# Attention and a gated MLP on one core: a planner that counts the loads of q and k, and the broadcast of the reciprocals, for longer

## The chip, the cores and the metric

The kernel runs on one core of a Trainium2 chip. The metric is the device time of one execution in microseconds (us), as the median of several executions.

## The reference

Eight batches, eight heads, 576 positions, head size 64. The attention output goes straight into a gated MLP with a mixing over positions. Everything is 32-bit float. Cut to what matters:

```python
q_rot, k_rot = rotate(q), rotate(k)              # rotary embedding over 64 features
scores = matmul(q_rot, k_rot.T) / sqrt(64)
attn = exp(scores - max(scores)); attn /= sum(attn) + 1e-9
x = matmul(attn, v)                              # (8, 576, 512) after heads are joined
h = maximum(x @ w_in, 0); u, v = halves of h     # w_in 512 x 1024
v_n = (v - mean) / sqrt(var + 1e-6)
v_s = einsum('ts,bsd->btd', w_spatial, v_n) + b_spatial
out = (u * v_s) @ w_out
```

## The kernel before

**Tiling.** Two heads of a batch make a *pair*; there are 32 pairs, four to a batch, and after each four an MLP for their batch. Each value that a matmul needs in more precision is split into a rounded high part and the rest, its low part. The scores of a pair are nine tiles of 128 queries by 576 keys (`sc`), each followed by a negated row maximum on VectorE (`nmx`, line 563), an exponential on ScalarE (`e`, line 565) whose row sums go to `sums`, transposes (`tp`) and products with v (`pv`). Pair 0 is treated whole in plain 32-bit float (`prepare_whole`, line 552), pairs 1 to 3 have split scores but plain values (`attention_plain`), and pairs 4 to 31 are split throughout (`attention`).

**The preparation of a pair** (`prepare`). Two loads bring q and k with their swapped halves into two `stage` buffers (`st`, line 409, issued at line 306 like every transfer). Then come, for each of q and k, two products with the rotary tables (line 401, tables `tabq` and `tabs`) and their sum (line 405), the rounding on ScalarE (line 309) and the low part (line 312). Ten transfers inside the chip, the *stack*, then put the parts in place for the scores (`qs`, `ks`, `qz`). There are only two stage buffers, so the loads of a pair wait until the last stack transfer of the pair before has read them; and `qs`, `ks`, `qz` exist once, so a stack waits until TensorE has finished the scores of the pair before.

**The end of a pair** (`normalise`). Once all nine columns of sums are there, VectorE takes the reciprocal (line 711) and transposes it (`rt`, line 712); `put` writes it to DRAM in four transfers; `get` reads it back broadcast to 128 partitions in three (`rb`, line 714). GpSimd then multiplies `x32`, the pair's attention output, by `rb` (line 716). The MLP reads the result.

**The order of the work** comes from a planner that runs when the kernel is built (`Program.run`). Each operation carries a cost in ns for its engine and a key, and a list of what it waits for. The planner walks through time: when an engine is free, it takes, among the operations that are ready and find a buffer, the one with the lowest key. A result counts as there after the cost, the engine's own latency (`LATENCY`, 1700 ns for a transfer, 118 for VectorE, 200 for TensorE) and `late`, an extra that is 0 unless it is set. All transfers share one queue in the plan, one after the other. `pair_op` marks operations that either GpSimd or VectorE may take, VectorE with 10 added to the key (`STEAL`), and in the plan the two never run such operations at the same time; pairs whose key is under `EARLY` (140) offer nearly all of theirs to both. At one instant VectorE is looked at before GpSimd. Only the order that comes out is used: on the chip each engine runs its list in that order and waits at each instruction for what it needs.

**Costs that the prediction uses**: loads of k, the table and q of pair 0 at 1450 each and v at 910, then pair 1's two loads at 1640 each; `turn_k` at 2280, the two parts of `turn_q` at 736 and 1336, a score tile of pair 0 at 1056, `nmx` at 665; a rotary product or sum 668 on VectorE and 1378 on GpSimd; `put` 2600, `get` 2000.

Weight decoding (`decode`) fills VectorE between the pairs up to about 110 us: six VectorE operations and two on ScalarE for each of twelve weight blocks.

Of the kernel before, what the change touches and what calls it, by code (L numbers as in the profile page):

```python
# [29 lines left out]
PE, ACT, DVE, POOL, DMA = "pe", "act", "dve", "pool", "dma"  # L30
LATENCY = {PE: 200, ACT: 142, DVE: 118, POOL: 95, DMA: 1700}
TO_PE = 105
LATE = 1500
SLOTS = {
    "stage": 2, "lk": 1, "vraw": 2, "vs": 2, "e2": 4, "e1": 2, "eh": 7, "rb": 1, "x32": 1, "xg": 7, "m": 4,
    "small": 3, "nmx": 3, "rt": 2, "sc": 2, "pv": 1, "pm": 3,
# [32 lines left out]
K_INV, K_GET, K_X, K_XHI, K_XLO = 15, 21, 26, 24, 27  # L69
# [37 lines left out]
class Program:  # L107
# [5 lines left out]
    def op(self, eng, ns, key, f, r=(), w=(), new=(), port=False):  # L113
        return self.either({eng: ns}, key, lambda e: f(), r, w, new, port)
# [23 lines left out]
    def run(self, make):  # L138
        free = {p: list(range(n)) for p, n in SLOTS.items()}
        ready = {e: [] for e in LATENCY}  # L140

        own = dict.fromkeys(SLOTS, 0)
        for o in self.ops:
# [80 lines left out]
def tile_attention_gated_mlp(  # L224
# [33 lines left out]
    op = prog.op  # L258
    vec = {DVE: nc.vector, POOL: nc.gpsimd}

    def pair_op(n, key, f, pieces=1, first=POOL, **kw):

        costs = {POOL: pool_ns(n) + 150 * (pieces - 1)}
        if first == DVE:
            costs = {DVE: dve_ns(n) + 68 * (pieces - 1)} if key < EARLY else {DVE: dve_ns(n) + 68 * (pieces - 1), **costs}
        elif key < EARLY:
            costs[DVE] = dve_ns(n) + 68 * (pieces - 1)
        prog.either(costs, key, lambda e: f(vec[e]), **kw)
# [36 lines left out]
    def load(dst, src):  # L305
        nc.sync.dma_start(out=dst, in_=src)

    def round_hi(hi, src):
        nc.scalar.activation(hi, src, AF.Copy)  # L309

    def rest_lo(eng, lo, src, hi):
        eng.tensor_tensor(out=lo, in0=src, in1=hi.bitcast(F32), op=ALU.subtract)  # L312
# [68 lines left out]
    def prepare(i):  # L381
        b, hp = pairs[i]
        key = 20 * i
        if i < WHOLE:
            return prepare_whole(i, b, hp, key)
        st = [Buf("stage", [P, 2 * S + TW], F32, f"st{i}_{j}") for j in range(2)]
        lk = Buf("lk", [P, TW + S], F32R, f"lk{i}")
        vr = Buf("vraw", [P, NQ, 2, D], F32, f"vr{i}")
        vs = Buf("vs", [P, NQ, 2, 2, D], F32R, f"vs{i}")
        prepped.append((lk, vr if i < PLAIN else vs))  # L390

        def hi(j, rows=slice(0, P)):

            return st[j][rows, S:2 * S + TW * j].bitcast(F32R)

        def lo_q(e):
            rest_lo(e, st[0][:, :S].bitcast(F32R), st[0][:, :S], hi(0))

        def rope(j, part, eng):
            cols = slice(S * part.start, S * part.stop)  # L400
            f = lambda e: e.tensor_tensor(out=st[j][:, cols], in0=st[j][:, cols], in1=(tabs if j else tabq)[:, cols], op=ALU.mult)  # L401
            pair_op(S * (part.stop - part.start), key - K_ROPE, f, first=eng, r=["tabs" if j else "tabq"], w=[(st[j], c) for c in range(part.start, part.stop)])

        def rope_sum(j, eng):
            f = lambda e: e.tensor_tensor(out=st[j][:, :S], in0=st[j][:, :S], in1=st[j][:, S:2 * S], op=ALU.add)
            pair_op(S, key - K_SUM, f, first=eng, r=[(st[j], 1)], w=[(st[j], 0)])

        for j in range(2):
            o = op(DMA, 1640, key - K_LOAD, lambda j=j: load(st[j][:, :2 * S], qk[b, hp, j].rearrange("p c n -> p (c n)")), w=[(st[j], 0), (st[j], 1)], new=[st[j]])
            o.late = LATE if i >= 4 else 0  # L410
        op(DMA, 910, key - K_LOAD + 1, lambda: load(vr.tile, v[b, hp]), w=[vr], new=[vr])
        for j, eng, part in ROPE0 if b == 0 else ROPE:
            if part is None:
                rope_sum(j, eng)
            else:
                rope(j, slice(*part), eng)
        op(ACT, 573, key - K_HIQ, lambda: round_hi(hi(0), st[0][:, :S]), r=[(st[0], 0)], w=[(st[0], 1)])
        pair_op(S, key - K_LOQ, lo_q, r=[(st[0], 1)], w=[(st[0], 0)])

        def hi_k():  # L420
            round_hi(hi(1)[:, TW:], st[1][:, :S])
            round_hi(hi(1)[:, :TW], st[1][:, 4 * P:S])

        def lo_k(e):
            rest_lo(e, lk[:, TW:], st[1][:, :S], hi(1)[:, TW:])
            rest_lo(e, lk[:, :TW], st[1][:, 4 * P:S], hi(1)[:, :TW])

        op(ACT, 720, key - K_HIQ, hi_k, r=[(st[1], 0)], w=[(st[1], 1)])
        pair_op(S + TW, key - K_LOK, lo_k, pieces=2, r=[(st[1], 0), (st[1], 1)], w=[lk], new=[lk])
        for a in range(2):  # L430
            own = slice(64 * a, 64 * a + 64)
            oth = slice(64 - 64 * a, P - 64 * a)
            qd, kd = qs[a][:, a * TW:a * TW + S], ks[a]
            zd = qz[:, a * S:a * S + S]
            for dst, rows, j, part, tok in (
                (qd, own, 0, 1, ("qs", a, 0)), (kd, own, 1, 1, ("ks", a, 0)), (kd, oth, 1, 1, ("ks", a, 1)),
                (zd, own, 0, 1, ("qz", a)), (qd, oth, 0, 0, ("qs", a, 1)),
            ):
                op(DMA, 650, key - (K_STACK2 if a else K_STACK), lambda dst=dst, rows=rows, j=j, part=part, own=own: load(dst[rows, :].bitcast(F32), hi(j, own).bitcast(F32) if part else st[j][own, :S]), r=[(st[j], part)], w=[tok])
        if i < PLAIN:  # L440
            return
        op(ACT, 627, key + K_V, lambda: round_hi(vs[:, :, :, 0, :], vr.tile), r=[vr], w=[(vs, 0)], new=[vs])
        pair_op(2 * NQ * D, key + K_VLO, lambda e: e.tensor_tensor(out=vs[:, :, :, 1, :], in0=vr.tile, in1=vs[:, :, :, 0, :].bitcast(F32), op=ALU.subtract), r=[vr, (vs, 0)], w=[(vs, 1)])
# [245 lines left out]
    def normalise(i, sm, x32, key):  # L689
        rt = Buf("rt", [P, 32], F32, f"rt{i}")  # L690
        rb = Buf("rb", [P, S], F32, f"rb{i}")
        x = Buf("xg", [P, 2 * S + TW], F32R, f"x{i}")
        xs.append(x)
        need = [("sums", i % 2, c) for c in range(9)]

        def put():
            for j in range(4):
                load(rt.scratch[:, 32 * j:32 * j + 32], rt[32 * j:32 * j + 9, :])

        def get():  # L700
            row = rt.scratch.rearrange("t p -> (t p)").rearrange("(o n) -> o n", o=1)
            load(rb[0:64, :], row[:, :S].to_broadcast([64, S]))
            load(rb[64:P, 4 * P:], row[:, S:S + TW].to_broadcast([64, TW]))
            load(rb[64:P, :4 * P], row[:, S + TW:].to_broadcast([64, 4 * P]))

        def low(e):
            rest_lo(e, x[:, S + TW:], x32.tile, x[:, :S])
            rest_lo(e, x[:, S:S + TW], x32[:, 4 * P:], x[:, 4 * P:S])

        op(ACT, 100, key + K_INV, lambda: nc.scalar.activation(sm[:, 0:9], sm[:, 0:9], AF.Copy, bias=1e-9), w=need)  # L710
        op(DVE, 130, key + K_INV, lambda: nc.vector.reciprocal(out=sm[:, 0:9], in_=sm[:, 0:9]), w=need)
        op(DVE, 125, key + K_INV, lambda: nc.vector.transpose(out=rt.tile, in_=sm), r=need, w=[rt], new=[rt])
        op(DMA, 2600, key + K_INV, put, r=[rt], w=[(rt, 1)])
        op(DMA, 2000, key + K_GET, get, r=[(rt, 1)], w=[rb], new=[rb])
        whole = [(x32, c) for c in range(len(CHUNKS))]
        pair_op(S, key + K_X, lambda e: e.tensor_tensor(out=x32.tile, in0=x32.tile, in1=rb.tile, op=ALU.mult), r=[rb], w=whole)  # L716
        op(ACT, 573, key + K_XHI, lambda: round_hi(x[:, :S], x32.tile), r=whole, w=[(x, 0)], new=[x])
        pair_op(S, key + K_XLO, low, pieces=2, r=[*whole, (x, 0)], w=[(x, 1)])
# [142 lines left out]
    for n in range(0):  # L861
        idle = Buf("pv", None, None, f"idle{n}")
        wide = lambda: ident.rearrange("p (o n) -> p o n", o=1).to_broadcast([P, 4, P])
        op(PE, 1600, 10000 + n, lambda idle=idle: nc.tensor.matmul(idle.tile.rearrange("p (c n) -> p c n", c=4), lhsT=ident, rhs=wide(), start=True, stop=True), r=["ident"], w=[idle], new=[idle])
    prepare(0)
    for c in range(4):
        decode(DEC_V[c], win, (1, c), w_in[c * P:(c + 1) * P, 2 * HF:4 * HF])
# [7 lines left out]
    for i in range(len(pairs)):  # L875
        if i:
            prepare(i)
        (attention_plain if i < PLAIN else attention)(i)
        if i % NP == NP - 1:
            mlp(i // NP)  # L880
# [68 lines left out]
```

## Time and profile before

| | |
|---|---|
| median of 3 executions | 967.62 us (966.43 to 967.69) |
| the profiled execution | 965.91 us, its span 964.0 us |
| TensorE busy | 933.5 us, 97% of the span |
| ScalarE, VectorE, GpSimd busy | 738.9, 670.5, 576.8 us |
| granted TensorE clock | 1.0 throughout |

The span goes from the first to the last instruction; some 1.9 us of the profiled execution lie outside it. PE is TensorE's matmuls, PEld its weight loads, DVE is VectorE, ACT ScalarE, POOL GpSimd, and SPq the queue that issues all transfers. TensorE's busy time counts overlapping matmuls once.

### The profile page before, as it was taken

The page shows a single profiled execution, that of the slowest core. Times are in us where ns is not written, and L with a number is a line of the kernel's source. Part 1 is how long each engine was busy: PE and PEld are TensorE (multiplying, and loading weights), DVE is VectorE, ACT ScalarE, POOL GpSimd, SP SyncE. Part 2 cuts the span into 40 slices and gives each one's busy share as a digit, 9 for nine tenths or more (in the row PEclk, how much of TensorE's full clock was granted, in tenths as well). Part 3 has the DMA queues.
Part 4 walks back from the last instruction along what each step waited for, and adds up shares of the span by engine and source line. Part 5 has one row for each costly group of instructions (what it writes and reads, how often), then busy time and mean ns, then how long its engine had stood idle before and what let it go on. Part 6 is the DMA issues. An engine that isn't in the chain of part 4 may idle for free.

```text
span 964.0 us, 19475 instructions
## 1 busy us (share of the span) xinstructions
PE 933.5 (97%) x6614; PEld 853.2 (89%) x6614; DVE 670.5 (70%) x1478; ACT 738.9 (77%) x1840; POOL 576.8 (60%) x504
## 2 busy tenths in 40 slices
PE   4988999999999999999999999999999999999998
PEld 2555689999899989999899998999889998999998
DVE  6999797766866677666776668676686766866331
ACT  4887798777987779777897779877798678976452
POOL 5566454566767657775765766666586775672121
PEclk9999999999999999999999999999999999999999
DMA  7786643455354654346444444445524455430101
GB/s 269 243 244 173 167 123 109 131 135 144 93 141 112 168 145 105 108 115 175 126 131 126 115 148 117 127 122 152 145 76 132 125 165 146 104 88 13 62 1 50
DMA packets 56037, 124.64 MB, mean 129 GB/s; under 512 B 13185, under 2 KB 13441, under 8 KB 55938
## 3 DMA queue, kind: packets, MB, share of 16 engines
q1 hardware_dynamic: 55938, 123.40, 46.4%
q8 instruction: 53, 0.87, 0.4%
q14 instruction: 46, 0.38, 0.1%
HBM read 66.03 MB, written 9.58 MB: 78 GB/s over the span
## 4 chain that ended last, share of the span: by engine, by line
PE 71%; ACT 14%; DVE 8%; DMA 3%; issue 2%; POOL 1%; SPq 1%; ACTq 0%; DVEq 0%
PE pc L791 12%; PE sc L542 12%; PE pv L606 11%; PE tp L582 11%; PE pd L806 10%; PE pb L773 9%; ACT e L565 4%; PE pa L750 4%; DVE nmx L563 2%; ACT eh L593 2%; ACT vv L837 2%; DVE el L312 1%; PE pv L679 1%; ACT vv L824 1%; ACT st L309 1%
## 5 line engine op out<-in xcount | busy, mean ns | idle before, releaser
L593 ACT ACTIVATE eh<-tp 128x384 fp32r<-128x384 f32 (+1 forms) x504 | 217.8, 434 | 87.7 <-PE tp L582 70.8
L312 DVE TENSOR_TENSOR el<-tp,eh 128x384 fp32r<-128x384 f32 x336 | 185.5, 553 | 99.6 <-ACT eh L593 87.6
L563 DVE TENSOR_REDUCE nmx<-sc 128x1 f32<-128x576 f32 x288 | 214.9, 749 | 39.9 <-PE sc L542 35.2
L565 ACT ACTIVATE e<-sc,nmx 128x576 f32<-128x576 f32 x288 | 213.4, 741 | 36.5 <-DVE nmx L563 33.7
L582 PE MATMUL tp<-ident,e 128*128 128x128 f32 (+1 forms) x1176 | 195.8, 273 | 3.2 <-DVE eh L312 1.3
L401 POOL TENSOR_TENSOR st<-st,tabq 128x576 f32<-128x576 f32 x58 | 82.1, 1432 | 150.1 <-DMA st<-in_qk_dram 115.8
L582 PEld LDWEIGHTS tp<-ident,e 128*128 128x128 f32 (+1 forms) x1176 | 145.3, 138 | 19.0 <-issue 4.0
L606 PE MATMUL pv<-eh,vs 128*128 128x384 f32 (+1 forms) x560 | 154.4, 316 | 0.4 <-ACT x L685 0.2
L791 PE MATMUL pc<-wsp,vn 128*128 128x288 f32 x768 | 143.3, 303 | 0.5 <-DVE u L853 0.5
L773 PE MATMUL pb<-x,wi 128*128 128x288 f32 x768 | 141.8, 306 | 1.0 <-DVE eh L312 0.7
L806 PE MATMUL pd<-g,wo 128*128 128x288 f32 x768 | 141.3, 303 | 0.0
L542 PE MATMUL sc<-ks,qs 128*128 128x288 f32 x620 | 132.1, 302 | 2.3 <-ACT e L565 2.2
L750 PE MATMUL pa<-wi,x 128*128 128x512 f32 x448 | 133.0, 407 | 0.9 <-POOL x L312 0.5
L542 PE MATMUL sc<-lk,qz 128*128 128x288 f32 x558 | 119.5, 295 | 0.0
L791 PEld LDWEIGHTS pc<-wsp,vn 128*128 128x128 f32 x768 | 114.9, 189 | 2.8 <-DVE u L853 0.9
L806 PEld LDWEIGHTS pd<-g,wo 128*128 128x128 f32 x768 | 114.2, 189 | 3.2 <-DVE el L312 0.2
L773 PEld LDWEIGHTS pb<-x,wi 128*128 128x128 f32 x768 | 112.0, 189 | 4.5 <-PE pb L773 1.3
L606 PE MATMUL pv<-el,vs 128*64 128x384 f32 (+1 forms) x448 | 113.7, 294 | 0.0
L542 PEld LDWEIGHTS sc<-ks,qs 128*128 128x128 f32 x620 | 99.7, 188 | 13.3 <-ACT e L565 5.8
L606 PEld LDWEIGHTS pv<-eh,vs 128*128 128x128 f32 x560 | 97.7, 188 | 6.5 <-DVE x L621 1.6
L716 POOL TENSOR_TENSOR x<-x,rb 128x576 f32<-128x576 f32 x32 | 45.8, 1431 | 84.4 <-DVE x L621 81.0
L312 DVE TENSOR_TENSOR eh<-tp,eh 64x256 fp32r<-64x256 f32 (+1 forms) x168 | 59.8, 356 | 48.8 <-ACT eh L593 25.2
(173 smaller groups left out, 1538.2 us busy)
## 6 DMA issues: line engine op xcount, KB each, us to landing
st<-in_qk_dram SPq DMA_DIRECT2D x64, 576.0 KB
ks<-st SPq DMA_DIRECT2D x124, 160.0 KB
qs<-st SPq DMA_DIRECT2D x124, 144.0 KB
vr<-in_v_dram SPq DMA_DIRECT2D x32, 320.0 KB
qz<-st SPq DMA_DIRECT2D x62, 144.0 KB
out_dram<-ob SPq DMA_DIRECT2D x31, 288.0 KB
ws<-in_w_spT_dram SPq DMA_DIRECT2D x2, 576.0 KB
tabs<-in_tab_dram SPq DMA_DIRECT2D x1, 576.0 KB
```

The lines of the kernel that those rows point to most:

```text
L312: eng.tensor_tensor(out=lo, in0=src, in1=hi.bitcast(F32), op=ALU.subtract)
L401: f = lambda e: e.tensor_tensor(out=st[j][:, cols], in0=st[j][:, cols], in1=(tabs if j else tabq)[:, cols], op=ALU.mult)
L542: nc.tensor.matmul(pt[:, c * 512:c * 512 + HALF], lhsT=lhsT, rhs=rhs[:, k0 + c * HALF:k0 + (c + 1) * HALF], start=(n == 0), stop=(n == len ...
L563: op(DVE, 665, key + K_MAX, lambda: nc.vector.tensor_reduce(out=nmx.tile, in_=tops(), op=ALU.max, axis=AX.XY, negate=True), r=[pt], w=[nmx ...
L565: op(ACT, 730, key + K_EXP, lambda: nc.scalar.activation(e[:, e0:e0 + S].rearrange("p (c n) -> p c n", c=2), tops(), AF.Exp, bias=nmx.tile ...
L582: nc.tensor.transpose(out=tp[:e.shape[1], m * P:m * P + P], in_=e, identity=ident)
L593: nc.scalar.activation(h, p, AF.Copy)
L606: nc.tensor.matmul(pv[0:rows, c1:c2], lhsT=vs[:, kt, h, vp, :], rhs=part[:, c1:c2], start=(kt == 0 and n == 0 and c1 == 0), stop=last)
L750: nc.tensor.matmul(pm.tile, lhsT=lhsT, rhs=win[1, d][:, j, :], start=(d == 0 and n == 0), stop=(d == 3 and n == len(todo) - 1))
L773: nc.tensor.matmul(pm[:, :HALF], lhsT=win[0, d][:, i, f * P:(f + 1) * P], rhs=x[d][:, at:at + HALF], start=(d == 0 and n == 0), stop=(d == ...
L791: nc.tensor.matmul(pm[:, :HALF], lhsT=lhsT, rhs=rhs, start=(t == 0 and n == 0), stop=(t == 4 and n == 1))
L806: nc.tensor.matmul(pm[:, :HALF], lhsT=wout[d,][:, i, m * P:(m + 1) * P], rhs=gs[d][:, at:at + HALF], start=(d == 0 and n == 0), stop=(d == ...
```

## The change

`late` is set to `LATE` (1500 ns) for the loads of q and k of every pair, where it was 0 for pairs 1 to 3 (pair 0 does not go through this line); and the broadcast `get` is given `late` 1000 ns for every pair, where it had none. No instruction is added or removed: only the planner's reckoning differs, and with it the order.

```diff
+LATE_GET = 1000
...
             o = op(DMA, 1640, key - K_LOAD, lambda j=j: load(st[j][:, :2 * S], qk[b, hp, j].rearrange("p c n -> p (c n)")), w=[(st[j], 0), (st[j], 1)], new=[st[j]])
-            o.late = LATE if i >= 4 else 0
+            o.late = LATE
...
-        op(DMA, 2000, key + K_GET, get, r=[(rt, 1)], w=[rb], new=[rb])
+        o = op(DMA, 2000, key + K_GET, get, r=[(rt, 1)], w=[rb], new=[rb])
+        o.late = LATE_GET
```

## Rows read from the trace of the kernel before

**Rows 1.** Busy time by stretch: us from:to, length, then each engine, clock, DMA.

```profile
0.00:20.00 20.00, 7.11 (x21) 4.60 (x22) 13.00 (x18) 7.38 (x14) 8.62 (x20) 1.00 0.79 286
20.00:40.00 20.00, 18.90 (x91) 10.76 (x89) 17.75 (x29) 14.83 (x36) 13.07 (x11) 1.00 0.81 250
40.00:60.00 20.00, 18.52 (x125) 11.64 (x124) 18.55 (x32) 17.98 (x46) 10.07 (x10) 1.00 0.76 205
60.00:80.00 20.00, 17.02 (x110) 10.00 (x107) 18.37 (x33) 16.57 (x41) 13.30 (x12) 1.00 0.80 234
80.00:100.00 20.00, 17.29 (x114) 10.46 (x112) 18.58 (x33) 16.90 (x42) 14.43 (x12) 1.00 0.59 163
100.00:160.00 60.00, 56.76 (x376) 47.28 (x376) 52.03 (x115) 50.47 (x128) 28.39 (x23) 1.00 0.53 148
...
200.00:900.00 700.00, 697.91 (x5085) 662.60 (x5084) 488.24 (x1115) 562.13 (x1411) 448.54 (x382) 1.00 0.46 124
```

**Rows 2.** Timeline from 9 to 17 us: start, duration, engine, line, idle before.

```profile
9.27 2.30 PE L552 MATMUL sc<-kf,st 64*128 64x288 f32 x8 [9.27 <-DVE st L474]
10.11 0.56 DVE L474 TENSOR_TENSOR st<-st 128x384 f32<-128x384 f32 x1
10.31 1.61 POOL L401 TENSOR_TENSOR st<-st,tabq 128x576 f32<-128x576 f32 x1 [5.23 <-DMA st<-in_qk_dram]
10.59 1.95 DVE L401 TENSOR_TENSOR st<-st,tabq 128x576 f32<-128x576 f32 x1
12.47 1.41 DVE L563 TENSOR_REDUCE nmx<-sc 128x1 f32<-128x576 f32 x2
13.31 0.74 ACT L565 ACTIVATE e<-sc,nmx 128x576 f32<-128x576 f32 x1 [6.16 <-DVE nmx L563]
13.80 0.74 DVE L401 TENSOR_TENSOR st<-st,tabs 128x576 f32<-128x576 f32 x1
14.19 3.01 PE L552 MATMUL sc<-kf,st 64*128 64x288 f32 x8 [2.63 <-ACT e L565]
```

**Rows 3.** TensorE from 22 to 30 us, and the chain of work there.

```profile
26.55 2.19 PE L552 MATMUL sc<-kf,st 64*64 64x288 f32 x8
29.35 0.50 PE L542 MATMUL sc<-ks,qs 128*128 128x288 f32 x2
```

```profile
23.25 3.09 DMA qs<-st
...
26.41 6.04 DMA st<-in_qk_dram
```

**Rows 4.** ScalarE's last rounding for pair 2's keys, and SP's stack behind it.

```profile
41.69 0.84 ACT L309 ACTIVATE st<-st 128x576 fp32r<-128x576 f32 x2
```

```profile
47.12 0.48 SPq L306 DMA_DIRECT2D qs<-st  x1
```

**Rows 5.** Timeline, pair 3's preparation: SP, GpSimd, TensorE.

```profile
56.87 1.37 SPq L306 DMA_DIRECT2D st<-in_qk_dram  x2
...
74.76 2.40 SPq L306 DMA_DIRECT2D ks<-st  x4
```

```profile
60.81 2.80 POOL L401 TENSOR_TENSOR st<-st,tabq 128x576 f32<-128x576 f32 x2 [6.99 <-DMA st<-in_qk_dram]
...
65.45 1.42 POOL L405 TENSOR_TENSOR st<-st 128x576 f32<-128x576 f32 x1
...
66.92 1.41 POOL L716 TENSOR_TENSOR x<-x,rb 128x576 f32<-128x576 f32 x1
...
71.64 1.40 POOL L401 TENSOR_TENSOR st<-st,tabs 128x576 f32<-128x576 f32 x1
...
78.95 0.53 PE L542 MATMUL sc<-ks,qs 128*128 128x288 f32 x2
```

**Rows 6.** The reciprocals of pairs 0 and 1 transposed, and x32 finished.

```profile
32.56 0.20 DVE L712 STREAM_TRANSPOSE rt<-sums 128x32 f32<-128x32 f32 x1
...
51.88 0.21 DVE L712 STREAM_TRANSPOSE rt<-sums 128x32 f32<-128x32 f32 x1
```

```profile
46.64 0.72 ACT L685 ACTIVATE x<-pv 64x192 f32<-64x192 f32 x3
```

```profile
66.12 0.72 ACT L685 ACTIVATE x<-pv 64x192 f32<-64x192 f32 x3
```

**Rows 7.** What GpSimd's product with the reciprocals waited for, whole span.

```profile
L716 POOL TENSOR_TENSOR x<-x,rb 128x576 f32<-128x576 f32 x32 | 45.8, 1431 | 84.4 <-DVE x L621 81.0 <-ACT x L685 3.3
```

**Rows 8.** Rotary products and sums that VectorE took before 160 us.

```profile
L405 DVE TENSOR_TENSOR st<-st 128x576 f32<-128x576 f32 x6 | 4.7, 782 | 0.6 <-POOL st L401 0.6
L401 DVE TENSOR_TENSOR st<-st,tabq 128x576 f32<-128x576 f32 x4 | 4.2, 1052 | 0.0
...
L401 DVE TENSOR_TENSOR st<-st,tabs 128x576 f32<-128x576 f32 x3 | 3.4, 1148 | 0.0
```

## The prediction

> **What bounds the kernel now.** I read the table of busy time by stretch first. From 200 to 900 us TensorE is busy for 697.91 of 700 us, at a granted clock of 1.0 [rows 1]. There TensorE is the bound, and no order of the other engines can give back more than the 2.1 us that are missing. The time that an order can win or lose lies ahead of that. From 0 to 160 us TensorE is busy for 7.11 + 18.90 + 18.52 + 17.02 + 17.29 + 56.76 = 135.6 us, so it idles for 24.4 us, of which 9.27 us are the wait for the very first scores [rows 1, 2]. Some 15 us remain. From 40 to 100 us VectorE is busy for 18.55 + 18.37 + 18.58 = 55.5 of 60 us, 92%, with weight decoding between the reductions [rows 1]; TensorE there waits for evictions and exponentials that stand behind that work. Whatever is saved or lost up to 160 us should go to the end undiminished, since TensorE is full from then on.
>
> The change touches the plan at two places only: the loads of pairs 1, 2 and 3, and the broadcast of every pair. I take them in turn, working the planner's order out by hand from its costs, and taking durations from the trace.
>
> **The broadcast: 0.** In the plan `rb` counts as there 2600 + 1700 + 2000 + 1700 = 8000 ns after the transpose of the reciprocals, and 9000 after the change, when the transfer queue is free. The product of line 716 also needs `x32`. For pair 0 the transpose starts at 32.56 and `x32` is finished at 46.64 + 0.72 = 47.36, 14.8 us later; for pair 1 it is 51.88 and 66.84, 15.0 us [rows 6]. The product never waited for `rb`: its idle time of 84.4 us goes to `x32` in 81.0 and 3.3 [rows 7]. So 9.0 us still end before 14.8, the product becomes ready at the same instant, and nothing is reordered. The cover is some 5.8 us; if the queue delayed the two transfers by that much in the plan, up to the extra 1.0 us would show, once for such a pair, on GpSimd. I count 0.
>
> **Pair 1's loads: a gain of about 1.0 us.** In the plan the first load of pair 1 starts after 3 x 1450 + 910 = 5260 ns, and counts as there at 5260 + 1640 + 1700 = 8600, after the change at 10100. VectorE is free at 2900 + 1700 + 2280 + 736 + 1336 = 8952. The first score tile starts at 7616 + 118 + 105 = 7839 and its maximum is ready at 7839 + 1056 + 200 = 9095. So before, at 8952 the rotary product is the only thing ready, and VectorE takes it ahead of the maximum. The trace shows this order and its price: the product starts at 10.59, takes 1.95 us beside GpSimd's of 1.61, and the two maxima follow only at 12.47, while ScalarE has been idle for 6.16 us and TensorE then waits 2.63 us for the third tile [rows 2]. After the change the maximum goes first at 9095, and at 10100 (49 ns before the second maximum is ready, at 8895 + 1056 + 200 = 10151) VectorE takes a rotary product and then the second maximum.
>
> On the chip the first maximum can then start at about 10.67, where line 474 ends, and not at 12.47: 1.80 us sooner. The second starts after a rotary product that begins at about 11.4 and ends no sooner than GpSimd's, 11.92, plus 0.74 for the product itself, at 12.66; before, it started some 0.7 us into the 1.41 us of both, at 13.18: 0.5 us sooner. Score tiles take turns on two buffers, so one stream gains 1.8 and the other 0.5. The last plain tile runs at 26.55 to 28.74 and pair 1's first scores at 29.35 [rows 3]. I take 1.0 us, between the ends, nearer the slower stream, since both feed the same nine tiles in order. The bounds are 0, if TensorE catches up later and only idles elsewhere, and 1.8.
>
> The rule that bears on this comes from the Trainium skill, page "SBUF — State Buffer", section "Who interferes with whom": a VectorE instruction with two inputs in SBUF and a GpSimd instruction that reads SBUF exclude one another, and the later one blocks until the other is done. The trace agrees: 10.59 + 1.95 = 12.54 is GpSimd's end at 11.92 plus 0.62. By that rule alone, with a rotary product still between the two maxima, the gain would be the slower stream's 0.5 us.
>
> The rest of pair 1's preparation gets later by up to 1.5 us in the plan. On the chip the last stack transfer lands at 23.25 + 3.09 = 26.34, and pair 1's scores start at 29.35: 3.0 us of cover [rows 3]. I count 0; without the cover each us would count in full.
>
> **Pair 2's loads: 0.** They start when pair 1's stack has landed, at 26.41 the second, and take 6.04 us, against 1640 + 1700 in the plan [rows 3]. Pair 2's keys are rounded by 41.69 + 0.84 = 42.53 and the stack starts at 47.12, when TensorE lets go of the buffers [rows 4]. So 4.6 us of lateness are hidden. The extra 1.5 us in the plan push the rotary work back by at least as much, and I count 0.
>
> **Pair 3's loads: 0, between 0 and a loss of 3.1 us.** Here the chain has no slack: loads issued at 56.87, products from 60.81 on after 6.99 us of idle, the last product at 71.64, the stack of keys at 74.76, pair 3's scores at 78.95 [rows 5]. GpSimd works almost without a gap from 60.81 to 73. In the plan the products start 1.5 us later against the rest, and the product with the reciprocals of pair 1 (key 46, below their 52) can go ahead of one that it followed before: the sum of line 405 at 65.45 and the product at 66.92 change places. As long as GpSimd has the same work up to the last product, its end does not move. If GpSimd has to stand and wait for `x32`, which is there only at 66.84 [rows 6], it loses the time from 65.45 to 66.84, 1.4 us; with the low part of x pulled ahead as well, 3.1 us (1.41 + 1.69, the length of the two). I take 0, because pair 1's gain brings `x32` forward by about 1.0 of those 1.4 us.
>
> **The steady state: 0.** From pair 4 on the loads had their 1500 already, and TensorE has only 2.1 us to give.
>
> **Sum.** -1.0 us on the profiled execution: 965.91 - 1.0 = 964.9. That execution lies 1.71 us below the median of the runs, 967.62, so for the median I say 966.6.
>
> **The rivals.**
> *VectorE is relieved (faster).* Up to 160 us VectorE took 13 rotary products and sums, 12.3 us with their blocking [rows 8], while it was 92% busy. It takes one only when it happens to be free as the load comes in. Later loads move these instants, and each operation that falls to GpSimd takes 0.8 to 1.1 us off VectorE. GpSimd has room: 13.07 of 20 us busy from 20 to 40 [rows 1]. With the full 1.8 us of the first maximum and two such operations, 3.6 us: 964.0. Against it: the count may as well go up.
> *Pair 3 waits (slower).* GpSimd stands before the product of line 716 with pair 3's sum behind it. It decides from the point where `x32` comes more than 1.0 us after GpSimd's third product has ended. Price 1.4 to 3.1 us, with pair 1's gain used up by the same chain: 969.0 to 970.7, middle 969.9.
> *Nothing happens (same).* TensorE's 4 us per two plain tiles are set by the round through maximum and exponential, the first tiles' gain is lost in the next wait, and the time stays at 967.6.
>
> The Trainium skill, page "DMA: Bandwidth & Descriptors", section "Anatomy of one DMA — SWDGE (gpsimd) path", speaks against the change: it gives about 2.0 us plus the bytes over 436,000 per us, fitted on another issue path. My estimate from it for 589,824 bytes is 3.35 us, just what the plan counted without the extra, so that orders with the extra would leave engines idle beside data that has landed, 1.5 us for pair 3: 969.1. The trace shows 6.04 us for one such load and 60.81 - 56.87 = 3.9 for another [rows 3, 5], so I leave it inside the slower rival.
>
> **How the numbers follow.** About 0.2%, 1.94 us, is what a measurement can tell from no change here: below 965.7 is faster, above 969.6 slower. The forecast 966.6 (its own range 965.8 to 967.6) gets 0.33 and nothing-happens 0.12, both within 0.2%: 0.45. VectorE relieved gets 0.32, since 15 us of idle time stand open to a better order and VectorE is the fullest engine there. Pair 3's wait, with other stalls of its kind in the 100 us in which lists are reshuffled, gets 0.23. The range reaches from 963.0, past the faster rival's 964.0, to 970.6, the slower rival's upper price.
>
> **What would show it.** Right: `nmx` of line 563 near 10.7 us and ahead of any VectorE line 401; the third score tile near 12.4; pair 1's first scores before 29.0; line 716 in the same place among its neighbours from pair 4 on; 200 to 900 us unchanged. Wrong: VectorE's count of lines 401 and 405 far from 13 (faster or slower); pair 3's first scores later than 79 us against a line 716 that idles; a different pattern in the batches after 200 us, which would mean that the plan settled into another rhythm and that my zero for the steady state does not hold.

## The result and the profile after

The kernel after the change takes 970.25 us (median of 10 executions, 968.99 to 971.52), the kernel before 967.61 us beside it. The ratio is 1.003, 95% interval 1.0021 to 1.0040: slower by 0.3%. That lies inside the predicted range (963.0 to 970.6) and on the side that had 0.23; the forecast was 966.6, a gain of 1.0 us. The profiled execution takes 970.19 us, its span is 968.1. Three executions, 1023.12 us with 250 ns, 1133.04 with 500 ns and 2310.19 of the kernel before, were slow ones and are left out of every median and ratio in this document.

Busy time by stretch, the kernel after, with the columns of [rows 1]:

```profile
0.00:20.00 20.00, 8.72 (x21) 4.84 (x21) 11.11 (x16) 7.58 (x14) 10.60 (x22) 1.00 0.78 295
20.00:40.00 20.00, 19.70 (x87) 11.61 (x88) 16.34 (x28) 14.65 (x35) 13.67 (x12) 1.00 0.78 225
40.00:60.00 20.00, 17.09 (x116) 11.08 (x117) 19.11 (x34) 17.69 (x44) 10.37 (x10) 1.00 0.76 208
60.00:80.00 20.00, 16.71 (x98) 10.06 (x95) 18.34 (x31) 15.65 (x39) 9.76 (x8) 0.89 0.83 256
80.00:100.00 20.00, 17.99 (x117) 12.29 (x115) 17.43 (x30) 16.12 (x40) 12.19 (x10) 0.94 0.42 121
100.00:160.00 60.00, 54.91 (x354) 43.73 (x352) 49.38 (x109) 48.97 (x121) 30.52 (x25) 1.00 0.50 136
...
200.00:900.00 700.00, 698.69 (x5087) 663.34 (x5088) 489.45 (x1115) 562.47 (x1413) 452.73 (x386) 1.00 0.46 124
```

From 200 to 900 us nothing has changed: 698.69 us busy against 697.91. The loss lies ahead of 200 us, and the largest gap in TensorE's work there is from 100 to 160 us, 54.91 against 56.76. Between 60 and 100 us TensorE's granted clock (1.0 is its full speed) is below 1.0; that is one fall to half, taken up below.

The start, timeline from 9 to 16 us (start, duration, engine, line; lines stand one later than before up to 711, two from there on):

```profile
9.35 2.30 PE L553 MATMUL sc<-kf,st 64*128 64x288 f32 x8 [9.35 <-DVE st L475]
...
11.68 0.76 DVE L564 TENSOR_REDUCE nmx<-sc 128x1 f32<-128x576 f32 x1 [0.92 <-PE sc L553]
...
12.35 1.63 DVE L402 TENSOR_TENSOR st<-st,tabq 128x576 f32<-128x576 f32 x1
...
13.91 0.74 DVE L564 TENSOR_REDUCE nmx<-sc 128x1 f32<-128x576 f32 x1
...
15.74 0.76 DVE L564 TENSOR_REDUCE nmx<-sc 128x1 f32<-128x576 f32 x1 [1.09 <-PE sc L553]
```

The first maximum does go ahead of the rotary product, as worked out. But it waits 0.92 us for its score tile and starts at 11.68, not 10.67. The gain over [rows 2] is 0.79 us.

Rotary products and sums that VectorE took before 160 us, to be held against [rows 8], and the product with the reciprocals, against [rows 7] (count, busy us, mean ns, idle before):

```profile
L406 DVE TENSOR_TENSOR st<-st 128x576 f32<-128x576 f32 x4 | 3.8, 949 | 0.0
L402 DVE TENSOR_TENSOR st<-st,tabq 128x576 f32<-128x576 f32 x3 | 3.1, 1047 | 0.8 <-DMA st<-in_qk_dram 0.8
...
L402 DVE TENSOR_TENSOR st<-st,tabs 128x576 f32<-128x576 f32 x1 | 0.7, 746 | 0.0
```

```profile
L718 POOL TENSOR_TENSOR x<-x,rb 128x576 f32<-128x576 f32 x31 | 44.3, 1430 | 85.5 <-DVE x L622 77.8 <-ACT x L686 7.8
```

VectorE has 8 of them where it had 13, 7.6 us instead of 12.3. What the faster rival needed has happened, and the kernel is slower all the same. The idle time of the other line goes to `x32` and never to `rb`, as before.

GpSimd's list at pair 4's preparation, timeline of the kernel after:

```profile
84.11 2.80 POOL L402 TENSOR_TENSOR st<-st,tabq 128x576 f32<-128x576 f32 x2 [8.98 <-DMA st<-in_qk_dram]
86.85 1.43 POOL L402 TENSOR_TENSOR st<-st,tabs 128x576 f32<-128x576 f32 x1
88.22 1.42 POOL L406 TENSOR_TENSOR st<-st 128x576 f32<-128x576 f32 x1
92.65 1.41 POOL L718 TENSOR_TENSOR x<-x,rb 128x576 f32<-128x576 f32 x1 [3.00 <-ACT x L686]
94.02 1.41 POOL L402 TENSOR_TENSOR st<-st,tabs 128x576 f32<-128x576 f32 x1
...
100.66 1.41 POOL L406 TENSOR_TENSOR st<-st 128x576 f32<-128x576 f32 x1
```

Here is the picture of the slower rival, one pair later than it was put: GpSimd stands 3.00 us before line 718 (716 before) with products and a sum of the next pair behind it. Pair 4's sum of keys, which VectorE did at 96.49 us before the change, now starts at 100.66. Pair 4's first maximum moves from 104.22 to 108.90; of these 4.7 us, 2.2 are left against a profile of the old order in which the clock fell as well (below). It was tempting to stop here. The runs that move this chain show that it is not the cause.

### The profile page after: what moved, and what is told of

It is laid out like the page before. It is cut to its first block, busy times and chain, and to the rows that moved or that the text cites. A ratio compares the mean times of both kernels' runs of the same rounds, so it can differ in the third digit from the quotient of the medians.

```text
span 968.1 us, 19487 instructions
## 1 busy us (share of the span) xinstructions
PE 937.9 (97%) x6614; PEld 856.6 (88%) x6614; DVE 671.0 (69%) x1479; ACT 740.4 (76%) x1841; POOL 575.9 (59%) x502
## 4 chain that ended last, share of the span: by engine, by line
PE 74%; ACT 14%; DVE 8%; issue 2%; DMA 1%; SPq 0%; ACTq 0%; DVEq 0%
PE sc L543 12%; PE pc L793 12%; PE pv L607 11%; PE pd L808 11%; PE tp L583 11%; PE pb L775 9%; ACT e L566 4%; PE pa L752 4%; DVE nmx L564 3%; ACT eh L594 2%; ACT vv L839 2%; DVE el L313 1%; PE sc L553 1%; PE pv L680 1%; ACT st L310 1%
## 5 line engine op out<-in xcount | busy, mean ns | idle before, releaser
L402 POOL TENSOR_TENSOR st<-st,tabq 128x576 f32<-128x576 f32 x59 | 84.2, 1443 | 151.8 <-DMA st<-in_qk_dram 123.4
L313 POOL TENSOR_TENSOR g<-u,g 128x288 fp32r<-128x288 f32 x64 | 51.6, 813 | 70.1 <-ACT g L310 67.1
```

## The experiments

Each was timed beside the kernel before, in 4 to 12 executions. Ratios are to that kernel as it ran beside them.

| run | what it is | median us | ratio, 95% interval |
|---|---|---|---|
| e_get | the broadcast alone | 967.81 | 1.0005 (0.9994 to 1.0015) |
| e_late1 | loads of pair 1 alone | 967.23 | 0.9998 (0.9986 to 1.0011) |
| e_late2 | loads of pair 2 alone | 968.04 | 1.0007 (0.9995 to 1.0019) |
| e_late3 | loads of pair 3 alone | 972.10 | 1.0042 (1.0027 to 1.0058) |
| f_late1 | e_late1 with filler matmuls | 978.67 | 1.0107 (1.0088 to 1.0125) |
| f_after | after with filler matmuls | 979.75 | 1.0123 (1.0104 to 1.0143) |
| g_late3_x1 | e_late3, one product moved back | 970.29 | 1.0035 (1.0021 to 1.0049) |
| g_after_x2 | after, one product moved back | 970.44 | 1.0032 (1.0018 to 1.0045) |
| h_after_sum | after, pair 4's sum forward | 970.41 | 1.0034 (1.0018 to 1.0050) |
| h_after_k4 | the same and its transfers | 969.58 | 1.0025 (1.0015 to 1.0035) |

### The parts one by one

```diff
-            o.late = LATE if i >= 4 else 0
+            o.late = LATE if i >= 4 or i == 1 else 0     # e_late1; e_late2, e_late3: 2, 3
```

e_get leaves this line and sets `late` of the broadcast alone.

> Only the broadcast counts 1000 ns longer; the loads of pairs 1 to 3 as before. The prediction's step says 0: the product of line 716 waits for x32 and never for rb, so no instruction changes place and the ratio to before should be 1.000 (within 0.1%). A rival in which the broadcast is what costs expects +2.6 us, the whole of the change.

> Only pair 1's loads count 1500 ns longer. Theory A: the loss begins in pair 1, whose preparation is really late (in the changed kernel the maxima of pair 1 run 1.3 us behind before), and is carried: +1.3 us or more, with the first maximum near 11.7 us. Theory B: the loss is made where pair 3 and pair 4 are prepared, on GpSimd's list: then pair 1 alone gives 0 to +1.0 us. Theory C, the clock of TensorE: a loss only if the granted clock falls below 1.0 before 160 us.

> Only pair 2's loads count 1500 ns longer. My step said 0, since 4.6 us of lateness are hidden. Theory A: 0 to +0.5 us. Theory B: up to +2.0 us if the lists of pairs 3 and 4 change as they do in the changed kernel, else 0. Theory C: a loss only with a fall of the granted clock.

> Only pair 3's loads count 1500 ns longer. Theory A: 0. Theory B: this is the chain without slack, so +2 to +4 us, with pair 4's first maximum later than 104.2 us by as much. Theory C: a loss only with a fall of the granted clock.

With the broadcast alone, each engine's list is the same as before the change, and so is the time: that edit is worth nothing, and e_get serves below as a second profile of the old order. Pair 1 and pair 2 alone are not told from no change. Pair 3 alone costs more than the whole change. The parts don't add up: -0.2, +0.7 and +4.2 parts in a thousand against 3.0 for all. So each part is not a stall of its own that can be priced by itself.

For pair 1 the clock hides something. In e_late1 the granted clock fell in all twelve executions (mean 0.996 or 0.995); of the 29 of the kernel before that were timed beside it, 14 stayed at 1.0. At the same 0.996 e_late1 takes 967.09 us (eleven executions) against 968.47 (twelve). Sorted by clock, pair 1's later loads are thus some 1.4 us faster, and the fall takes that back. No run held the clock up in this order, so that rests on sorting executions alone.

### Is it the clock?

An execution's mean clock is 0.996 where TensorE's granted clock has stood at half for some 6.8 us in all. In the profile of the kernel after this is from 75.6 on, behind a stretch in which TensorE was busy 3.19 of 5.5 us; busy time by stretch:

```profile
70.00:75.50 5.50, 3.19 (x14) 1.28 (x14) 5.25 (x11) 5.46 (x15) 2.84 (x3) 1.00 0.95 259
75.60:82.30 6.70, 6.08 (x22) 4.16 (x23) 3.95 (x7) 1.47 (x3) 0.00 (x0) 0.50 0.67 163
82.50:88.00 5.50, 5.38 (x37) 3.35 (x36) 5.50 (x10) 5.30 (x13) 3.89 (x3) 1.00 0.58 201
```

The profile of before has none, so the two profiles differ by it. To hold the clock up, four extra matmuls of `ident` were put behind each of the first four value products of the first chunk, in pairs 1 to 3, into columns of `pv` that are not read:

```diff
+                if i in (1, 2, 3) and c == 0 and kt < 4:
+                    for _ in range(4):
+                        nc.tensor.matmul(pv[:, 384:512], lhsT=ident, rhs=ident, start=False, stop=False)
```

> Only pair 1's loads late, with the same extra matmuls. In the runs so far this order has the clock at 0.996 every time and 967.5 us, where runs of the kernel before with that clock take 968.3 and with 1.0 take 966.4. Theory C: with the clock held at 1.0 this order takes 965.5 to 966, faster than before by 0.1 to 0.2%, and that is the gain of pair 1 that the prediction named. If the extra work only delays: 967.5 to 969.

> The changed kernel, its order unchanged, with four extra small matmuls of the identity after each of the first four value products of pairs 1 to 3, into columns that nobody reads, in gaps where TensorE waits for evictions (some 0.2 us each group member at most). Theory C: the granted clock stays at 1.0 up to 900 us and the time falls by 1.0 to 1.9 us, to 968.4 to 969.3. If the clock's fall costs nothing beyond the waits around it: 970.2 or up to 2 us more for the added work.

This told nothing: the fillers took 13.9 us of TensorE, far more than a fall costs. The clock did stay at 1.0 in all four executions of f_after, but not in f_late1 (0.996 and 0.997). The executions themselves tell more. Of 127 of the kernel before, 40 were at 1.0 (median 966.51 us) and 68 at 0.996 (968.26): such a fall goes with some 1.7 us and is common in the old order too. At the same 0.996 the kernel after takes 971.37 us (three executions), 3.1 us more; at 0.998 it takes 970.07 (six) against 966.99 (seven), again 3.1. The clock is not the difference between these two kernels.

The comparison at one clock in the profiles is that of after with e_get, 0.996 both, 2.1 us apart. Pair 8's first maximum, timeline of VectorE, in e_get and then in after:

```profile
214.13 0.69 DVE L564 TENSOR_REDUCE nmx<-sc 128x1 f32<-128x576 f32 x1
```

```profile
216.55 0.69 DVE L564 TENSOR_REDUCE nmx<-sc 128x1 f32<-128x576 f32 x1
```

The whole difference, 2.42 us here, is there by this point, and all of the rest runs alike. In the same pair of profiles pair 3's first maximum is still 1.88 us earlier in after (80.80 against 82.68), pair 4's is 2.23 us later.

### Is it pair 4's preparation?

First the product with the reciprocals was put behind the key products that it had stepped in front of: pair 1's behind pair 3's second key product in the order of e_late3, and pair 2's behind pair 4's in the order after.

```diff
+    mark[('x', 1)].behind = mark[('turn', 3, 1, 1)]     # g_late3_x1
+    mark[('x', 2)].behind = mark[('turn', 4, 1, 1)]     # g_after_x2
```

> The order with only pair 3's loads late (972.1 us), with one change of place: the product of pair 1 with its reciprocals comes out behind pair 3's second key product on GpSimd's list, not ahead of pair 3's sum. Theory B (GpSimd stands before that product, 2.23 us at 66.23, with pair 3's sum and key product behind it): the key product starts near 65.4 instead of 68.95, pair 3's first maximum comes 2 to 3 us sooner than 83.39, and the time falls to 969 to 970. If the wait costs nothing by itself, the time stays within 0.5 us of 972.1.

> The changed kernel's order (970.25 us), with the product of pair 2 with its reciprocals put behind pair 4's second key product on GpSimd. Theory B: GpSimd's wait of 3.00 us before it at 92.65 no longer holds the key product of 94.02, which starts near 89.6; three other operations still stand before pair 4's sum of keys, so that this moves by 1.4 us (100.66 to 99.3), pair 4's first maximum by 1.0 to 1.4 from 108.90, and the time to 968.9 to 969.3. If the chain of pair 4 is set elsewhere (ScalarE's list): within 0.4 us of 970.25.

The first fits neither forecast: 970.29 us, 1.8 below e_late3, with ratios of 1.0035 and 1.0042 whose intervals overlap. Pair 3's first maximum came 2.4 us sooner (80.96 against 83.39), but the mean clock of the two profiled executions differs as well (0.998 and 0.993). What the exchange of places is worth is left open; it is not the whole loss, since 1.0035 is still clear of 1. The second left the time where it was, 970.44 us: the key product moved from 94.02 to 90.11, but three other operations of GpSimd still stood ahead of the sum, which started at 100.84. So the sum itself was taken forward, directly behind that product, with its rounding on ScalarE (h_after_sum), and then the four `ks` transfers ahead of the write-back of the reciprocals as well (h_after_k4). All else in the order is that of after: an operation is issued once the planner's clock has passed the number beside it, and is skipped at its old place.

```diff
+    prog.early = [(84261, mark[('sum', 4, 1)], POOL), (86000, mark[('hik', 4)], ACT)]     # h_after_sum
...
+    prog.early = [(84261, mark[('sum', 4, 1)], POOL), (86000, mark[('hik', 4)], ACT), (86001, mark[('stack', 4, 'ks', 0, 0)], DMA), (86001, mark[('stack', 4, 'ks', 0, 1)], DMA), (86001, mark[('stack', 4, 'ks', 1, 0)], DMA), (86001, mark[('stack', 4, 'ks', 1, 1)], DMA)]     # h_after_k4
```

> The order after the change, but pair 4's sum of keys stands on GpSimd directly behind pair 4's second key product, ahead of the low part of x, the low part of q and the vs write, and ScalarE rounds the sum right behind; the transfers' order is left as it is. Theory 'pair 4's preparation': the sum starts near 95.4 us of the profiled span instead of 100.66, the first ks transfer near 102 (it still stands behind the write-back of the reciprocals), pair 4's first maximum near 107.4 instead of 108.90, and the time falls by 1 to 1.5 us to about 969. Rival 'the loss is elsewhere' (in pair 3's scores or in the later order): within 0.4 us of 970.25.

> As the kernel with the sum brought forward, and SyncE issues pair 4's four ks transfers ahead of the write-back of the reciprocals as well. Theory 'pair 4's preparation': first ks transfer near 99, pair 4's first maximum near 104.3 (that of the kernel before: 104.22), and most of the loss is gone: 966.3 to 967.8 us. If only half of it lies there, about 969. Rival 'the loss is elsewhere': within 0.4 us of 970.25.

Neither came out as that theory forecast. In h_after_sum the sum starts at 96.05, but the write-back of the reciprocals goes out only at 101.72, and `ks` with 103.33 is no earlier than after (103.50). In h_after_k4 the first `ks` transfer goes out at 95.82, 7.7 us sooner than after. Some 2.4 of these are the clock, which has not fallen by then in this profile: the product of line 718 (733 here) starts at 90.29 instead of 92.65. The median falls by only 0.7 us, with intervals that overlap, and at a mean clock of 0.998 nothing is left of it: 970.21 us (seven executions) against 970.07 (six). TensorE's timeline in h_after_k4 says why (its lines stand 15 later than after):

```profile
100.59 0.97 PE L767 MATMUL pa<-wi,x 128*128 128x512 f32 x3
...
102.91 0.95 PE L767 MATMUL pa<-wi,x 128*128 128x512 f32 x3
...
104.57 0.95 PE L767 MATMUL pa<-wi,x 128*128 128x512 f32 x3
105.36 0.43 PE L558 MATMUL sc<-ks,qs 128*128 128x288 f32 x2
```

and busy time by stretch of the same execution:

```profile
100.00:108.00 8.00, 8.00 (x51) 4.91 (x47) 5.46 (x10) 4.29 (x9) 0.00 (x0) 1.00 0.73 235
```

Pair 4's scores stand behind MLP products in TensorE's list, and TensorE is busy for 8.00 of these 8 us. In the kernel after, busy time by stretch and TensorE's timeline are:

```profile
100.00:110.00 10.00, 9.75 (x59) 5.72 (x57) 7.14 (x12) 6.14 (x14) 2.25 (x3) 1.00 0.64 172
```

```profile
100.41 0.55 PE L642 MATMUL tp_3b<-ident,e 128*128 128x128 f32 x3 [0.25 <-ACT et_2b L649]
...
107.73 0.43 PE L543 MATMUL sc<-ks,qs 128*128 128x288 f32 x2
```

TensorE is busy for 9.75 of the 10 us in which pair 4's keys are late there, and what it lacks is a wait of 0.25 us for ScalarE in pair 3's transposes. With the keys early the scores start 2.37 us sooner, at 105.36, no more than line 718's product gained by the clock (2.36). The plan has laid other work over the wait, and the lateness that the trace shows so plainly was covered. As a wait on the chip, pair 4's preparation falls as the cause. Where the plan puts pair 4's scores in TensorE's list is a part of the order that these two runs leave as it is.

What is left is the order as a whole. Where TensorE waited from 84 to 135 us, clock 1.0 in both; first after, then e_get (who waits for whom, us in total, times, longest):

```profile
PE pv L607 <- DVE x L622: 1.2, 1, 1.2
PE tp L583 <- DVE el L313: 0.9, 1, 0.9
PE tp L583 <- DVE eh L313: 0.7, 1, 0.7
PE tp_1a L642 <- ACT et_0b L649: 0.7, 1, 0.7
PE tp_2a L642 <- DVE et_1b L651: 0.7, 1, 0.7
...
```

```profile
PE sc L543 <- ACT e L566: 1.9, 3, 1.0
PE tp L583 <- DVE el L313: 0.9, 1, 0.9
PE tp_2b L642 <- ACT et_1b L649: 0.5, 1, 0.5
...
```

Each order has its own set of waits of about 1 us, for VectorE and ScalarE, at different instructions. In sum TensorE is busy for 23.86 + 21.64 = 45.50 of these 51 us in after and for 23.43 + 23.13 = 46.56 in e_get, busy time by stretch, after and then e_get:

```profile
84.00:110.00 26.00, 23.86 (x156) 14.98 (x153) 22.22 (x39) 20.34 (x50) 14.44 (x12) 1.00 0.46 122
110.00:135.00 25.00, 21.64 (x138) 16.80 (x137) 20.40 (x44) 19.94 (x52) 12.02 (x9) 1.00 0.58 170
```

```profile
84.00:110.00 26.00, 23.43 (x149) 15.24 (x150) 23.11 (x39) 21.15 (x52) 16.17 (x14) 1.00 0.61 183
110.00:135.00 25.00, 23.13 (x151) 18.69 (x150) 21.39 (x50) 20.90 (x54) 13.54 (x12) 1.00 0.52 147
```

Up to 110 us, where pair 4's keys are late, TensorE is busy no less in after than in the old order; the shortfall of 1.1 us in these 51 comes behind that.

### The number itself

A small change of one ready time can change which operation the planner takes next, and with it all its later choices, as when cards are dealt anew. If the change acts in that way, the time should not follow how late the loads are counted. If it acts by later loads, it should grow with the number. Only the number was changed, for pairs 1 to 3:

```diff
-            o.late = LATE
+            o.late = LATE if i >= 4 else 250     # d_250; and so on
```

> The kernel after the change with 250 ns instead of 1500 on the loads of pairs 1 to 3, a sixth of the change. Theory 'the order is dealt anew': how late a load is counted does not set the loss, any value deals another order of the whole first 130 us, good or bad; this one puts pair 4's first maximum later in the plan than before and ends later in it, so 969 to 972 us, as slow as the whole change or slower. Rival 'the later loads push a chain' (dose): a sixth of the loss, 968.0 at most.

> 500 ns instead of 1500. Theory 'dealt anew': this order has pairs 3 to 5 earlier in the plan than the kernel before and the same end, so 966 to 968 us, no loss or a small gain. Rival (dose): a third of the loss, 968.5.

> 1750 ns instead of 1500. Theory 'dealt anew': the plan's end is near that of the kernel before, so 967 to 968.5 us, less than the kernel after the change although every load is counted later. Rival (dose): 970.7 or more.

> 2000 ns instead of 1500. Theory 'dealt anew': a bad deal, the plan ends the latest of the four, 971 to 975 us, with 1750 ns some 4 us below it. Rival (dose): 971.1, 0.4 us from the kernel with 1750 ns.

Three of these came out in the range of the new deal, and 1750 ns half a microsecond under its own. The next four were chosen to break the theory: the smallest step, a neighbour of the change, and the values that the plan likes best.

> 50 ns instead of 1500 on the loads of pairs 1 to 3, a thirtieth of the change. Theory 'the order is dealt anew': even so small a number deals another order, whose plan ends late; 969 to 971.5 us, most of the loss. Rival (the loss grows with the number): 967.7, no change.

> 650 ns. Theory 'dealt anew': of 52 values from 0 to 2550, counted out in the kernel's own plan, this one ends first; 964 to 966.5 us, below both kernels. Rival (dose): 968.8.

> 1450 ns, 50 less than the change has. Theory 'dealt anew': the plan that ends last of the 52; 973 to 976 us. Rival (dose), and any theory in which the transfers' own lateness matters: within 0.5 us of the change's 970.25.

> 2350 ns, more than the change has. Theory 'dealt anew': the plan that ends second of the 52; 965 to 967 us, below the kernel before. Rival (dose): 971.5 or more.

| ns counted for pairs 1 to 3 | median us | ratio, 95% interval | pair 8's first maximum, us |
|---|---|---|---|
| 0 (e_get) | 967.81 | 1.0005 (0.9994 to 1.0015) | 214.13 |
| 50 | 969.00 | 1.0013 (0.9997 to 1.0030) | 217.08 |
| 250 | 970.89 | 1.0028 (1.0017 to 1.0040) | 216.02 |
| 500 | 966.38 | 0.9984 (0.9973 to 0.9995) | 212.78 |
| 650 | 964.60 | 0.9966 (0.9951 to 0.9980) | 212.61 |
| 1450 | 974.93 | 1.0068 (1.0048 to 1.0088) | 222.63 |
| 1500 (the change) | 970.25 | 1.0030 (1.0021 to 1.0040) | 216.55 |
| 1750 | 966.46 | 0.9988 (0.9979 to 0.9997) | 212.25 |
| 2000 | 974.88 | 1.0075 (1.0062 to 1.0088) | 220.58 |
| 2350 | 967.39 | 0.9992 (0.9978 to 1.0005) | 211.90 |

There is no dose. 1450 and 1500 ns are 4.7 us apart; 250 is slower and 1750 faster than before. Six of the eight ranges of the new deal held; 1750 came 0.5 us under its range and 2350 0.4 us over. 50 ns stands at the edge of its range and is not surely apart from before. The last column is the start of pair 8's first maximum in each profiled execution. In 16 of the 18 profiles without fillers, what comes after that point takes 752.8 to 754.6 us to the end of the execution. So the order of the first 210 us sets the time. The exceptions, e_late2 and d_2350, lose some 3 us in the later course; in d_2350 TensorE waits 1.59 us for VectorE at 679.7 and its clock falls once more behind that, as busy time by stretch shows (clock 0.83):

```profile
680.00:690.00 10.00, 8.70 (x46) 7.75 (x47) 4.76 (x9) 6.45 (x16) 4.06 (x4) 0.83 0.38 87
```

The spread is not one of the clock alone. At a mean clock of 0.998 the kernel before takes 966.99 us (seven executions), 650 ns 963.74 (four) and 2000 ns 974.88 (three). But with 50 and 250 ns much of the loss goes with the clock: 50 ns takes 967.51 at 1.0 (three) and 971.33 at 0.991 (four), and the eight executions with 250 ns all lie between 0.989 and 0.995. So the orders differ in how long the clock falls in them as well as in their waits.

The two ends of the table, timelines of VectorE in d_650 and d_1450:

```profile
212.61 0.69 DVE L564 TENSOR_REDUCE nmx<-sc 128x1 f32<-128x576 f32 x1
```

```profile
222.63 0.69 DVE L564 TENSOR_REDUCE nmx<-sc 128x1 f32<-128x576 f32 x1
```

With 650 ns the kernel takes 964.6 us: it beats the kernel before by 0.34%, and the one after by more. The plan's own end, which `Program.run` gives without the chip, told the good values from the bad ones. Against 0 it comes 1.8 us earlier for 650 and 1.1 earlier for 2350, level for 500, 0.5 later for 1750, 2.5 for 1500, 3.1 for 50, 3.8 for 250, 6.2 for 2000 and 7.2 for 1450. It is no exact price: for pair 1's loads alone it says 3.7 us later, and the chip showed no loss. Of the 51 values from 50 to 2550 in steps of 50, 49 end later in the plan than 0 does, and so a change of this number, in whatever direction it is meant, mostly loses.

## Why the prediction was wrong

**What bounds the kernel: right.** The result lies ahead of 200 us and goes to the end undiminished, and the steady state gives nothing.

**The broadcast, 0: right.** e_get has the old lists and the old time.

**Pair 1's loads, -1.0 us: right in the mechanism, too large.** The change of places came about, and TensorE waits for `e` before plain tiles 2.2 us in all instead of 4.0. The first maximum gained 0.79 us, not 1.8, since its score tile ends only at 11.6: I had taken VectorE's freedom as the bound where TensorE was. The second lost 0.78 (13.91 against 13.13, the second half of the pair of maxima in [rows 2]), where I had it win 0.5. Pair 1's first maximum came 1.33 us later than before; "before 29.0" for its scores was wrong, they start at 30.36. By itself this part is not told from zero: 0.9998. Sorted by clock it gains some 1.4 us, but the clock fell in every execution of that order, and the prediction had no term for the clock.

**Pair 2's loads, 0: not contradicted.** 1.0007, interval on both sides of 1.

**Pair 3's loads, 0: the step that failed.** Alone they cost 0.42%, some 4.1 us (interval 2.6 to 5.6), where I had put 0 with a bound of 3.1. It is not the clock alone: the one execution of e_late3 at 0.998 takes 972.44 us. I had followed one exchange of places on GpSimd and argued that its end does not move as long as the work up to there is the same. The change of a ready time does not stop at one exchange: each later choice of the planner depends on which engine happens to be free, so VectorE's share of rotary work, the places of the MLP products and the pairs from 4 on are dealt again.

**The sum** failed with it. It added terms each of which was priced against the old order, and the parts measured alone don't add. The forecast needed one more case: an order of the first 200 us that is new as a whole, with a spread of several us. The ten values above run from 964.6 to 974.9 us. I worked out single moves of the planner by hand and did not count the plan to its end: that end comes 2.5 us later with the change, and 2.6 us were measured.

**The rivals.** The slower rival had the side, the size (969.0 to 970.7) and a wait that is there to be seen, GpSimd before the product with `x32`; but for pair 4 it is not what costs: bringing forward what stood behind it changed nothing at the same clock (970.21 against 970.07 us). The faster rival's condition came true, 13 operations became 8, and gave no gain: VectorE's relief is only one part of a new order. My remark that 15 us of idle time stand open to a better order was right, as d_650 shows, and so was the note that the plan might reckon with data that is later or earlier than on the chip; but better reckoning of the loads is not what makes an order better. My estimate of 3.35 us for a load from the Trainium skill, page "DMA: Bandwidth & Descriptors", section "Anatomy of one DMA — SWDGE (gpsimd) path", is about how true the number is, and the time does not follow the number at all.

**What stays open.** Which waits make up the 2.4 us between the old order and the new one at equal clock is not settled one by one. Busy time does not hold them: from 0 to 160 us TensorE is busy for 135.12 us in after and 135.95 in e_get, 0.8 us apart. The lists differ everywhere between 15 and 160 us, and the intermediate marks cross (pair 3 earlier, pairs 4 and 5 later, pair 6 only 0.97 us later). No run grafts one engine's list alone onto the other order.

## What to carry to other kernels

A constant in a greedy planner is less a model of the chip than a seed: counting a load 50 ns later deals another order just as 2350 ns do, and its effect can't be priced move by move. Let the planner count its own end first, which here had the right side for the change and for most values; beyond that, forecast such a change as a draw from the spread of orders, and mind that the value in place may already be a good draw. Before keeping or refusing it, try several values on the chip, and compare executions at the same mean clock. A chain that comes late in the trace is a cause only where the engine that bounds the kernel has nothing to do there: look at its busy time in that stretch before moving the chain.

## What the runs showed of the hardware

TensorE's granted clock fell to half, 1.2 GHz, for some 6.8 us in the profiles of after and of e_get. In these it fell at 75.6 and at 71.2 us, behind stretches with TensorE busy for 3.19 of 5.5 and 2.98 of 5 us, and it came back with TensorE busy nearly throughout the fall (6.08 of 6.7 us in after). In the same kernel, the one before, executions with a mean clock of 0.996 take 1.7 us more than those at 1.0 (968.26 against 966.51 us), as much as the effects that were to be measured. How often it falls differs with the order: in 11 executions with 1750 ns it fell each time, in 12 with 650 ns three had no fall.
